# A gated delta rule in front of two expert layers on one Trainium2 core: small transfers on SyncE's queue moved or cut up, unit matrices by memset, more decode buffers, one input placed behind another

## The chip, the cores and the metric

One core of one Trainium2 chip. The metric is the device time of one execution in microseconds (us); the times shown are the median of several runs, and the profile is one execution on its own. Engines: PE is TensorE (PEld its weight loads), DVE VectorE, ACT ScalarE, POOL GpSimd, SP SyncE, which only issues transfers here.

## What is computed

```python
k_n = k / (norm(k) + 1e-6)                       # B=4, H=8, S=768, D=48
for t in range(S):                               # the recurrence, state is [B, H, D, D]
    y[t]  = q[t] @ state
    state = state + beta[t] * outer(k_n[t], v[t] - state @ k_n[t])
x = y as [3072, 384]
p = domain_probs / (domain_probs.sum(-1) + 1e-9)
x = sum over 4 experts e of  p[:, e] * (relu(x @ w1[e]) @ w2[e])       # inner width 1024
out = (sigmoid(x @ w_gate) * (x @ w_val)) @ w_out                      # inner width 1536
```

All inputs and the output are float32.

## The kernel before

**The recurrence in steps.** The sequence is cut into 12 steps of 64 tokens. Inside a step the recurrence is a triangular system, solved with the inverse of a unit triangular matrix per batch and head. Six inversions serve all steps (`INV`): each takes two steps at once, the first two in halves of 32 rows, the other four in full 64. An inversion starts from a unit matrix in `Xpp` (`l_init`, by a transfer from the input `xinit`), reads the triangles from DRAM into `Lpp` (`l_read`), runs pairs of DVE instructions (`itmp`, then `Xpp`; `inv_ops`) and stores its result (`x_out`, tiles `xs` or `xd`). A step's chain (`chain`, `plan_chain`) then reads it into `XT` (`x_in`; `off_in` reads the off-diagonal part into `Ld`), does small products on PE, and leaves its outputs in `YT`. From step 2 on `x_move` carries `YT` into `Y` by eight transfers on SP, two of 144 KB and six of 16 KB, and `x_split` turns `Y` into a rounded part and a rest (`xhi` on ACT, `xlo` on DVE).

**The expert layers.** Tokens go in six batches of two steps (512 columns). A batch passes the four experts ("m1" phases, 8 units of 128 inner columns each) and then the gated layer ("m2", 12 units). Every float32 product is three products of rounded parts. The weights come in tiles of 128x768 on SP (`w_load`, three `raw` buffers), are rounded on ACT and subtracted on DVE into `ws` (`w_split`, four buffers). `finish` multiplies the outputs of an expert with `pe`, the probabilities broadcast to all partitions (`load_p`, two buffers), and adds them in `ACC`, by an accumulating transfer on POOL's queue.

**Decode.** The gated layer's weights arrive as 36 tiles of 64-bit numbers and are turned into float32 once, in the time of the first batch: `dec_load` on SP, `dec_scale` on ACT, `dec_join` on DVE and POOL, `dec_store` on POOL's queue into `w2_d`. `dec_views` picks the buffers: five for the pairs, four (`n % 4`) for the results, all of them parts of tiles that are free at that time (`dec_a`, `dec_b`, `Lpp`, `Xpp`).

**The order.** All instructions are written out in one order by a planner. It counts a time T in planned microseconds that grows by PE's cost of each unit of the expert layers (1.94 for 9 products of 512 columns). Side work has due times on that scale: `plan` puts it into `todo`, decode and inversions go into `back`. `slot` and `fill` emit what is due between units; DVE work only as long as the planned DVE time is at most 2.8 ahead of PE's. Each engine and each queue then runs its own instructions in that order and waits by semaphores. So an instruction on SP that waits holds all transfers behind it, and a queue that waits for nothing runs ahead of PE. `Tile` also lets a transfer wait for the landing of an earlier one whose semaphore it takes over.

Due times around the change: W[1] = 194.6 is when the second batch begins and `g0` for its pair of later steps is W[1] - 116 = 78.6. `plan_norms` loads the keys of steps 4 and 5 from `g0` - 8 on, computes their norms (`norms`) at `g0` + 9 and at once moves them across partitions by four transfers of 4 KB on SP (`norm_move`, tile `nrm_v`). `plan_chain(2, ...)` begins at W[1] - 87 and reads its six inputs 14 before that, after forcing the rest of the second inversion. `x_move(3)` is due at 172.2, `x_split(3)` at 182.6, the read of the third inversion at 168.7. `load_p(n + 2)` follows the last product of phase n.

Of the kernel before, what the change touches and what calls it, by code (L numbers as in the profile page):

```python
# [18 lines left out]
B, H, S, D = 4, 8, 768, 48  # L19
DM = H * D  # L20
# [15 lines left out]
FLIP = 2  # L36
# [4 lines left out]
DEC0, DEC1 = 17.0, 162.0  # L41
# [11 lines left out]
INIT_AT = {}  # L53
_at = 0
for _ng, _n in sorted({inv_cut(r) for r in range(len(INV))}):
    INIT_AT[_ng, _n] = _at
    _at += _n * _n // _ng
# [62 lines left out]
def moe_delta_kernel(  # L120
# [12 lines left out]
    xinit: bass.AP,  # L133
# [112 lines left out]
    def dec_tiles():  # L246
        a = xp.tile([P, KT, 2 * STEP], F32, tag="xhi", name="dec_a").rearrange("p k c -> p (k c)")
        b = xp.tile([P, KT, 2 * STEP], F32, tag="xlo", name="dec_b").rearrange("p k c -> p (k c)")
        w = 2 * DM
        dec_mem.append([a[:, :w], a[:, w:], b[:, :w], Lflat[:, 2 * w : 3 * w], Lflat[:, 3 * w :]])  # L250
        t2 = [b[:, w:], Xflat[:, HC * HC : HC * HC + w]]
        dec_mem.append([t[:, o : o + DM] for o in (0, DM) for t in t2])
        dec_mem.extend([a, b, Lflat[:, 2 * w :]])

    def dec_views(n):
        r, t = dec_mem[0][n % 5], dec_mem[1][n % 4]
        pair = r.bitcast(I32).rearrange("p (a b) -> p a b", b=2)
        return r, pair[:, :, 0], pair[:, :, 1], t
# [226 lines left out]
    def l_init(r):  # L485
        ng, n = inv_cut(r)
        o = INIT_AT[ng, n]
        q[0].dma_start(
            out=x_view(r).rearrange("p j t -> p (j t)"), in_=xinit[:, o : o + n * n // ng]
        )  # L490
# [61 lines left out]
    def x_in(c):  # L552
        r, c2 = INV_OF[c]
        q[2] = nc.sync if c == 2 else q[0]
        xt = XT.rearrange("p h b t -> p (h b) t")
        for i in range(2):
            if INV[r][1]:
                for a in range(2):
                    src = xd_t[r][c2, a, i].rearrange("h b j t -> j (h b) t")
                    put(xt, i * C + a * HC, a * HC, HC, src)  # L560
            else:
                put(xt, i * C, 0, C, xd_t[r][c2, i].rearrange("h b j t -> j (h b) t"))

    def off_in(c):
        r, c2 = INV_OF[c]
        q[2] = nc.sync if c == 2 else q[0]
        if INV[r][1]:
            for bp in range(2):
                src = od_t[r][c2, :, :, bp].rearrange("i h j t -> j (i h) t")
                put(Ld.rearrange("p i h t -> p (i h) t"), bp * C, HC, HC, src)  # L570
# [83 lines left out]
    def x_move(c):  # L654
        dst = Y[c % 2].rearrange("p a f -> p (a f)").rearrange("p (k t) -> p k t", k=KT)
        for o in range(2):
            src = YT[o * C : o * C + D].rearrange("p a i t -> p a (i t)")
            nc.sync.dma_start(out=dst[o * D : (o + 1) * D], in_=src[:, 0:KT])
            for k in range(KT):
                p = 96 + 16 * o  # L660
                nc.sync.dma_start(out=dst[p : p + 16, k], in_=src[16 * k : 16 * k + 16, KT])
# [79 lines left out]
    def plan_norms(c, t):  # L741
        for n in range(2):
            box = []
            plan(t + 9.0 * n, lambda c=c + n, box=box: box.extend(norm_late(c, i) for i in range(2)))
            plan(t + 9.0 * n + 7.0, lambda box=box: [fn() for fn in box])
        plan(t + 17.0, lambda: norms(c, c + 2))

    def norms(c0, c1):
# [17 lines left out]
        if c0:  # L766
            norm_move(c0, c1)
# [172 lines left out]
    inv_done, read_at = [1], {}  # L940
# [29 lines left out]
    def plan_inv(r, tr, t0, t1):  # L970
# [15 lines left out]

        if r == 1:
            read_at[r] = -READ
        else:
            back["inv"].append((tr, "", read, lambda: l_done.issuperset(INV[r][0])))  # L990
# [5 lines left out]
    def plan_chain(c, t, gap):  # L996
# [3 lines left out]
        if c > 1 and c % 2 == 0:  # L1000

            def first():
                while inv_done[0] <= INV_OF[c][0]:
                    back["inv"].pop(0)[2]()
                x_in(c)
                off_in(c)

            plan(t - (14.0 if c == 2 else 13.0), first)
# [5 lines left out]
        if c >= FLIP:  # L1014
            plan(t1 - (2 if c < NC - 1 else 1) * gap + 4.0, lambda: x_move(c))
# [43 lines left out]
    def startup():  # L1059
# [23 lines left out]
        nc.gpsimd.memset(Xflat[:, : HC * HC], 0.0)  # L1083
        nc.gpsimd.memset(Xflat[:, : HC * HC : HC + 1], 1.0)
# [105 lines left out]
        norms(2, 4)  # L1190
        q[1] = None
# [33 lines left out]
    with tc.manual_schedule():  # L1225
# [15 lines left out]
        for k in range(1, NPAIR):  # L1241
# [4 lines left out]
            if k + 1 < NPAIR:  # L1246
                g0 = w - (161.0 if k > 1 else 116.0)
                plan_norms(2 * k + 2, g0 - 8.0)
# [5 lines left out]
            plan_tr(2 * k + 1, w - (TR2 if k > 1 else 12.0), 4.0)  # L1254
# [3 lines left out]
        for what, n, us in EVENTS:  # L1258
            kind, b, e, s0, ns = PHASES[n]
            part = unit_us(kind, ns) / (2 if kind == "m1" else 3)  # L1260
            if what == "b":
# [3 lines left out]
                if us[-1] == (NF1 if kind == "m1" else NF2) - 1 and n + 2 < len(PHASES):  # L1265
                    load_p(n + 2)
# [7 lines left out]
            slot()  # L1274

# [4 lines left out]
def _layouts(q, k, v, beta, moe_domain_probs, moe_w1, moe_w2, moe2_w_gate, moe2_w_val, moe2_w_out):  # L1280
# [43 lines left out]
    init = {}  # L1324
    for ng, n in sorted({inv_cut(r) for r in range(len(INV))}):
        x = np.zeros((ng, P // ng, n // ng, n), f)
        for g in range(ng):
            for j in range(n // ng):
                x[g, :, j, ng * j + g] = 1.0
        init[ng, n] = x.reshape(P, -1)  # L1330
    xinit = np.concatenate(list(init.values()), axis=1)
# [3 lines left out]
        "xinit": xinit,  # L1335
# [20 lines left out]
```

## Time and profile before

| | |
|---|---|
| runs (us) | 1453.33, 1451.38, 1453.0: median 1453.0 |
| profiled execution (us) | 1454.07 |
| its span, first to last instruction (us) | 1452.3 |
| instructions | 25287 |
| busy in the span | PE 1394.3 (96%), PEld 1147.2, DVE 1044.9, ACT 560.8, POOL 241.9 |
| mean granted TensorE clock | 0.974 |
| bytes moved | 246.24 MB, mean 170 GB/s |

The profile's page gives the span, what each engine did in it, and the chain of work that ended last. The trace behind it can be asked for stretches, for one engine's instructions in order of time, and for who ended each wait. A row `X <- Y` in a list of waits says that X stood idle until Y was done; a row of the timeline ends in the idle time before the instruction and its releaser. L148 is a helper through which all DVE instructions go, so DVE is told by tiles. The granted clock is the share of full speed that the chip's throttle gave PE.

### The profile page before, as it was taken

How to read it: one execution, taken by the hardware profiler on the slowest of the kernel's cores; microseconds unless marked ns; L12 is line 12 of the kernel's file. 1: busy time of each engine (PE TensorE's matmuls, PEld its weight loads, DVE VectorE, ACT ScalarE, POOL GpSimd, SP SyncE). 2: the span in 40 equal slices, each digit the busy share in tenths (PEclk: the TensorE clock that was granted, in tenths of full speed). 3: DMA queues.
4: the chain of work that ended last, by engine and by line, in shares of the span. 5: the costliest groups of instructions: out<-in, count | busy, mean ns of one | idle time of the engine just before them, and what ended most of it. 6: DMA issues, size and time to landing. Idle time of an engine off the chain costs nothing.

```text
span 1452.3 us, 25287 instructions
## 1 busy us (share of the span) xinstructions
PE 1394.3 (96%) x9939; PEld 1147.2 (79%) x9939; DVE 1044.9 (72%) x1809; ACT 560.8 (39%) x919; POOL 241.9 (17%) x297
## 2 busy tenths in 40 slices
PE   6879878898999999999999999999999999999998
PEld 5778766787878888878888878888888888888887
DVE  7559887885999677788777788767778755444553
ACT  3335443553332344332344333344433344333343
POOL 2314455660011200001210001210000210000000
PEclk6899998999999999999999999999999999999999
DMA  8876798778446865545775456775434663334331
GB/s 213 236 206 208 218 274 277 233 234 195 155 146 163 212 178 162 161 157 153 196 202 159 138 150 176 189 206 166 127 108 124 155 166 107 131 103 126 99 109 65
DMA packets 115510, 246.24 MB, mean 170 GB/s; under 512 B 38864, under 2 KB 43152, under 8 KB 113216
## 3 DMA queue, kind: packets, MB, share of 16 engines
q1 hardware_dynamic: 94512, 192.24, 43.6%
q0 software_dynamic: 16480, 50.43, 14.7%
q10 hardware_dynamic: 4400, 1.97, 0.6%
q8 instruction: 78, 1.28, 0.4%
q14 instruction: 40, 0.33, 0.1%
HBM read 202.10 MB, written 29.02 MB: 159 GB/s over the span
## 4 chain that ended last, share of the span: by engine, by line
PE 79%; DVE 9%; DMA 7%; issue 2%; ACT 1%; SPq 1%; ACTq 0%; DVEq 0%
PE ph L828 42%; PE acc L865 32%; DVE ws L148 2%; DVE Xpp L148 2%; DVE itmp L148 1%; DMA raw<-in_wp 1%; DMA kn<-in_kt 1%; DMA Y<-YT 1%; PE pu L596 1%; DVE hlo L148 1%; DMA Lpp<-ls 1%; DMA dec_a<-in_wp 1%; PE pk L596 1%; PE pg L373 1%; PE ps L676 1%
## 5 line engine op out<-in xcount | busy, mean ns | idle before, releaser
L828 PE MATMUL ph<-xhi,ws 128*128 128x512 f32 (+1 forms) x2064 | 631.7, 389 | 10.9 <-DVE ws L148 4.9
L865 PE MATMUL acc<-hhi,ws 128*128 128x512 f32 (+1 forms) x1632 | 499.9, 389 | 14.7 <-DVE ctmp L148 6.9
L828 PEld LDWEIGHTS ph<-xhi,ws 128*128 128x128 f32 x2064 | 382.9, 189 | 90.7 <-DVE ws L148 5.8
L828 PE MATMUL ph<-xlo,ws 128*128 128x512 f32 (+1 forms) x1032 | 396.6, 387 | 0.6 <-DVE xlo L148 0.6
L865 PEld LDWEIGHTS acc<-hhi,ws 128*128 128x128 f32 x1632 | 305.1, 190 | 81.1 <-ACT hhi L835 6.1
L148 DVE TENSOR_TENSOR ws<-raw,ws 128x768 fp32r<-128x768 f32 x308 | 302.8, 989 | 47.8 <-ACT ws L229 44.6
L865 PE MATMUL acc<-hlo,ws 128*128 128x512 f32 (+1 forms) x816 | 315.3, 386 | 2.2 <-DVE hlo L148 1.2
L835 ACT ACTIVATE hhi<-ph 128x512 fp32r<-128x512 f32 (+1 forms) x200 | 116.1, 581 | 426.3 <-PE ph L828 421.7
L229 ACT CAST ws<-raw 128x768 fp32r<-128x768 f32 x308 | 252.1, 830 | 62.3 <-DMA raw<-in_wp 51.3
L148 DVE SCALAR_TENSOR_TENSOR hlo<-ph,hhi 128x512 fp32r<-128x512 f32 (+1 forms) x200 | 133.2, 666 | 139.5 <-ACT hhi L835 139.4
L828 PEld LDWEIGHTS ph<-xlo,ws 128*128 128x128 f32 x1032 | 194.9, 189 | 41.4 <-DVE xlo L148 2.5
L865 PEld LDWEIGHTS acc<-hlo,ws 128*128 128x128 f32 x816 | 155.3, 190 | 33.7 <-DVE hlo L148 1.9
L148 DVE TENSOR_TENSOR itmp<-Xpp,Lpp 128x62 f32<-128x62 f32 (+29 forms) x344 | 161.8, 477 | 11.7 <-DMA Lpp<-ls 6.5
L148 DVE TENSOR_TENSOR Xpp<-Xpp,itmp 128x62 f32<-128x62 f32 (+29 forms) x344 | 158.1, 466 | 5.9
L844 ACT CAST hhi<-gv 128x512 fp32r<-128x512 f32 x72 | 44.7, 620 | 164.8 <-DVE gv L148 164.8
L148 DVE TENSOR_TENSOR gv<-ph,sg 128x512 f32<-128x512 f32 x72 | 49.7, 690 | 80.0 <-PE ph L828 76.2
L907 POOL DMA_DIRECT2D ACC<-ctmp x39 | 34.5, 1172 | 366.7 <-DVE ctmp L148 366.6
L148 DVE TENSOR_TENSOR hlo<-gv,hhi 128x512 fp32r<-128x512 f32 x72 | 52.7, 732 | 49.4 <-ACT hhi L844 49.4
L453 POOL DMA_DIRECT2D ld<-LP x12 | 8.1, 678 | 328.0 <-DVE LP L148 232.5
L842 ACT ACTIVATE sg<-ph 128x512 f32<-128x512 f32 x72 | 42.9, 596 | 41.0 <-PE ph L828 40.9
L148 DVE TENSOR_TENSOR ctmp<-acc,pe 128x512 f32<-128x512 f32 (+1 forms) x57 | 35.4, 655 | 10.1 <-PE acc L865 9.3
L581 POOL TENSOR_TENSOR V<-V,nrm_v 128x384 f32<-128x384 f32 x22 | 21.6, 1069 | 42.2 <-DMA V<-in_vt 17.9
(170 smaller groups left out, 927.8 us busy)
## 6 DMA issues: line engine op xcount, KB each, us to landing
raw<-in_wp SPq DMA_DIRECT2D x200, 384.0 KB, 3.3
raw<-w_d SPq DMA_DIRECT2D x108, 384.0 KB, 3.4
ACC<-ctmp POOLq DMA_DIRECT2D x33, 256.0 KB, 5.8
KQ<-in_kg SPq DMA_DIRECT2D x7, 896.0 KB, 7.1
Lpp<-ld POOLq DMA_DIRECT2D x8, 768.0 KB, 14.3
pe<-p_d SPq DMA_DIRECT2D x23, 256.0 KB, 4.7
dec_a<-in_wp SPq DMA_DIRECT2D x15, 384.0 KB, 4.3
Lpp<-in_wp SPq DMA_DIRECT2D x14, 384.0 KB, 6.0
```

The costliest lines, as they stand in the source:

```text
L148: return fn(*args, **kw)
L229: nc.scalar.copy(out=w[:, 0], in_=t)
L373: nc.tensor.matmul(out=pg[i][b * C : (b + 1) * C, j], lhsT=src[b][ROWS[i], 0, h], rhs=src[b][ROWS[i], :, h], start=True, stop=True,)
L581: nc.gpsimd.tensor_tensor(out=V[:, b], in0=V[:, b], in1=nrm_v[:, 2 * c + b].unsqueeze(2).to_broadcast([P, H, D]), op=ALU.mult,)
L596: nc.tensor.matmul(out=ps[r][HALVES[k], h], lhsT=lhsT, rhs=rhs, start=True, stop=True)
L676: nc.tensor.matmul(out=ps[C:112, h], lhsT=KI[0:112, 0, i, h], rhs=rhsA[:, i, h], start=True, stop=True)
L828: nc.tensor.matmul(out=res[q], lhsT=lt, rhs=rt, start=(k == 0 and j == 0), stop=(k == KT - 1 and j == 2))
L835: nc.scalar.activation(out=hh, in_=res[0], func=AF.Relu)
L842: nc.scalar.activation(out=sg, in_=res[0], func=AF.Sigmoid)
L844: nc.scalar.copy(out=hh, in_=gv)
L865: nc.tensor.matmul(out=acc_t[d][:, :w], lhsT=lt, rhs=rt, start=(u == 0 and j == 0), stop=(u == nf - 1 and j == 2),)
L907: nc.gpsimd.dma_start(out=a, in_=t, accum_op=ALU.add)
```

## The change

- `l_init`: the unit matrix of an inversion is written by one memset of zeros and one or two strided memsets of ones on POOL, in place of a transfer; the input `xinit` goes, and with it `INIT_AT`.
- `dec_views`: from tile 8 on the results go round nine buffers, five of them parts of `YQ1`, which step 1 has done with by then.
- `plan_norms`: the first load of keys is due 4 earlier (`g0` - 12), the second stays; `norm_move` leaves `norms` and is due at `g0` + 23 (at the start it follows `norms` as before).
- `plan_chain`, step 2: the second inversion is forced at 30 before the chain in place of 14, and the six inputs (four `XT`, two `Ld`) go on SP one by one, from 23 before the chain on, 2.6 apart.
- `x_move`: four pieces 1.4 apart, the two large transfers first, then the small ones, three and three.
- `plan_inv`: the third inversion's read (`l_init` and `l_read` on POOL's queue) is emitted only once the last piece of `x_move(3)` is emitted and 4 us of PE's planned time have passed.
- `x_split(3)` is due 3 later, 9 in place of 12 before the batch.
- `load_p(n + 1)` follows unit 3 of phase n, for n from 1 on.

```diff
-FLIP = 2
+FLIP, MOVE = 2, 4.0
-DEC0, DEC1 = 17.0, 162.0
+DEC0, DEC1, MORE = 17.0, 162.0, 8
...
+        y = YQ1.rearrange("p a i h t -> p (a i h t)")
+        dec_mem.append([y[:, o : o + DM] for o in range(0, 5 * DM, DM)] + dec_mem[1])
...
-        r, t = dec_mem[0][n % 5], dec_mem[1][n % 4]
+        r, t = dec_mem[0][n % 5], dec_mem[1][n % 4] if n < MORE else dec_mem[5][(n - MORE) % 9]
...
     def l_init(r):
         ng, n = inv_cut(r)
-        o = INIT_AT[ng, n]
-        q[0].dma_start(
-            out=x_view(r).rearrange("p j t -> p (j t)"), in_=xinit[:, o : o + n * n // ng]
-        )
+        w = P // ng
+        nc.gpsimd.memset(Xflat[:, : n * n // ng], 0.0)
+        for g in range(ng):
+            nc.gpsimd.memset(Xflat[g * w : (g + 1) * w, g : n * n // ng : n + ng], 1.0)
...
     def x_move(c):
         dst = Y[c % 2].rearrange("p a f -> p (a f)").rearrange("p (k t) -> p k t", k=KT)
-        for o in range(2):
-            src = YT[o * C : o * C + D].rearrange("p a i t -> p a (i t)")
-            nc.sync.dma_start(out=dst[o * D : (o + 1) * D], in_=src[:, 0:KT])
+        srcs = [YT[o * C : o * C + D].rearrange("p a i t -> p a (i t)") for o in range(2)]
+
+        def most(o):
+            nc.sync.dma_start(out=dst[o * D : (o + 1) * D], in_=srcs[o][:, 0:KT])
+
+        def rest(o):
+            p = 96 + 16 * o
             for k in range(KT):
-                p = 96 + 16 * o
-                nc.sync.dma_start(out=dst[p : p + 16, k], in_=src[16 * k : 16 * k + 16, KT])
+                nc.sync.dma_start(out=dst[p : p + 16, k], in_=srcs[o][16 * k : 16 * k + 16, KT])
+            moved[c] = pe_at[0]
+
+        return [lambda o=o, fn=fn: fn(o) for fn in (most, rest) for o in range(2)]
...
-            plan(t + 9.0 * n, lambda c=c + n, box=box: box.extend(norm_late(c, i) for i in range(2)))
-            plan(t + 9.0 * n + 7.0, lambda box=box: [fn() for fn in box])
-        plan(t + 17.0, lambda: norms(c, c + 2))
+            plan(t + 13.0 * n, lambda c=c + n, box=box: box.extend(norm_late(c, i) for i in range(2)))
+            plan(t + 13.0 * n + 7.0, lambda box=box: [fn() for fn in box])
+        plan(t + 21.0, lambda: norms(c, c + 2))
+        plan(t + 35.0, lambda: norm_move(c, c + 2))
...
-        if c0:
-            norm_move(c0, c1)
...
+        def ready():
+            return l_done.issuperset(INV[r][0]) and (r > 2 or pe_at[0] > moved.get(3, 1e9) + MOVE)
+
-            back["inv"].append((tr, "", read, lambda: l_done.issuperset(INV[r][0])))
+            back["inv"].append((tr, "", read, ready))
...
-                x_in(c)
-                off_in(c)
-
-            plan(t - (14.0 if c == 2 else 13.0), first)
+                if c > 2:
+                    x_in(c)
+
+            def one(n):
+                q[2] = nc.sync
+                put(*(x_parts(c) + off_parts(c))[n])
+
+            plan(t - (30.0 if c == 2 else 13.0), first)
+            for n in range(6 if c == 2 else 0):
+                plan(t - 23.0 + 2.6 * n, lambda n=n: one(n))
...
-            plan(t1 - (2 if c < NC - 1 else 1) * gap + 4.0, lambda: x_move(c))
+            for n, fn in enumerate(x_move(c)):
+                plan(t1 - (2 if c < NC - 1 else 1) * gap + 4.0 + 1.4 * n, fn)
...
-        nc.gpsimd.memset(Xflat[:, : HC * HC], 0.0)
-        nc.gpsimd.memset(Xflat[:, : HC * HC : HC + 1], 1.0)
+        l_init(0)
...
+        norm_move(2, 4)
...
-                plan_norms(2 * k + 2, g0 - 8.0)
+                plan_norms(2 * k + 2, g0 - 12.0)
...
-            plan_tr(2 * k + 1, w - (TR2 if k > 1 else 12.0), 4.0)
+            plan_tr(2 * k + 1, w - (TR2 if k > 1 else 9.0), 4.0)
...
-                if us[-1] == (NF1 if kind == "m1" else NF2) - 1 and n + 2 < len(PHASES):
-                    load_p(n + 2)
...
+            if us[0] == 3 and 0 < n < len(PHASES) - 1:
+                load_p(n + 1)
```

`x_parts` and `off_parts` are the new lists from which `x_in` and `off_in` issue, with the same sources and targets as before.

## Rows read from the trace of the kernel before

**Rows 1.** Stretches: width; busy PE, PEld, DVE, ACT, POOL; granted clock; DMA share, GB/s.

```profile
207.00:219.00 12.00, 7.61 (x25) 5.84 (x26) 11.90 (x16) 3.94 (x7) 11.16 (x11) 0.86 0.97 240
239.00:253.00 14.00, 9.81 (x26) 6.55 (x25) 10.70 (x16) 5.69 (x11) 6.74 (x8) 0.63 0.56 195
275.00:284.00 9.00, 5.81 (x47) 4.69 (x43) 5.75 (x7) 6.66 (x13) 8.55 (x12) 0.81 0.89 295
341.00:352.00 11.00, 6.39 (x19) 4.76 (x18) 4.94 (x9) 4.08 (x6) 0.00 (x0) 0.69 0.95 216
100.00:350.00 250.00, 224.27 (x1759) 183.67 (x1758) 193.18 (x325) 117.61 (x212) 121.76 (x137) 0.95 0.77 233
350.00:475.00 125.00, 124.14 (x648) 100.85 (x648) 118.64 (x212) 43.93 (x69) 11.74 (x16) 1.00 0.54 155
525.00:1450.00 925.00, 922.52 (x5804) 757.46 (x5802) 634.33 (x1000) 346.75 (x537) 71.26 (x92) 1.00 0.51 146
```

**Rows 2.** PE in order of time: start, us, instruction, [idle before it, releaser].

```profile
78.28 0.45 PE L596 MATMUL pk<-rhsA,KS 48*64 48x48 f32 x2 [4.64 <-DVE rhsB L148]
...
213.73 0.70 PE L865 MATMUL acc<-hhi,ws 128*128 128x512 f32 x2 [4.19 <-DVE ctmp L148]
...
242.09 1.19 PE L865 MATMUL acc<-hhi,ws 128*128 128x512 f32 x2 [2.31 <-DVE ws L148]
...
278.90 0.91 PE L828 MATMUL ph<-xhi,ws 128*128 128x512 f32 x2 [3.19 <-DVE ws L148]
...
346.16 1.22 PE L828 MATMUL ph<-xhi,ws 128*128 128x512 f32 x2 [4.61 <-ACT sg L842]
```

**Rows 3.** PE's waits from 100 to 350: total us, times, longest.

```profile
PE acc L865 <- DVE ws L148: 5.9, 4, 2.3
PE ph L828 <- DVE ws L148: 4.9, 2, 3.2
```

**Rows 4.** The chain that ended last, in order of time: start, us, what.

```profile
66.31 8.89 DMA Lpp<-ls
...
188.31 12.51 DMA kn<-in_kt
...
206.98 3.44 DMA dec_a<-in_wp
...
235.48 4.75 DMA w_d<-dec_b
...
269.59 6.48 DMA w_d<-Xpp
...
328.56 15.99 DMA Y<-YT
```

**Rows 5.** Waits of SP's queue (143:150, 195:205) and of ACT (whole span).

```profile
SPq L806 <- DVE itmp L148: 5.9, 1, 5.9
...
SPq L774 <- DVE norm_tmp L148: 8.0, 1, 8.0
...
ACT xhi L669 <- DMA Y<-YT: 11.2, 1, 11.2
...
ACT dec_b L268 <- DMA w_d<-dec_b: 2.7, 1, 2.7
```

**Rows 6.** Transfers issued: tiles, queue, count, KB each, median us to landing.

```profile
Xpp<-in_xinit SPq DMA_DIRECT2D x1, 512.0 KB, 7.2
```

**Rows 7.** Groups of POOL's instructions: count, busy us, mean ns, idle before.

```profile
L1083 POOL MEMSET Xpp<- 128x1024 f32 x1 | 1.0, 951 | 0.3 <-POOLq L1343 0.3
```

**Rows 8.** POOL in order of time, from 318 to 330.

```profile
323.64 0.56 POOL L488 DMA_DIRECT2D Xpp<-in_xinit  x1 [3.14 <-DMA w_d<-Xpp]
```

**Rows 9.** DVE in order of time, from 214 to 217.

```profile
215.55 2.65 DVE L148 TENSOR_TENSOR ws<-raw,ws 128x768 fp32r<-128x768 f32 x1
```

**Rows 10.** POOL in order of time, from 214 to 219.

```profile
215.73 3.15 POOL L581 TENSOR_TENSOR V<-V,nrm_v 128x384 f32<-128x384 f32 x2
```

**Rows 11.** Instructions that write or read `itmp`, by stretch: DVE busy (count), clock, DMA.

```profile
350.00:362.00 12.00, 5.74 (x18) 0.96 0.49 150
```

More of the change, by code (lines that the diff above doesn't have):

```diff
@@ L50, in inv_cut @@
     return ((2 if small else 4) // len(steps), HC if small else C)
[L53 to L57, printed above, removed]
 INV_OF = {c: (r, steps.index(c)) for r, (steps, _) in enumerate(INV) for c in steps}
@@ L132, in moe_delta_kernel @@
     mask: bass.AP,
-    xinit: bass.AP,
     out: bass.AP,
@@ L550, in put, with x_parts @@
         q[2].dma_start(out=t[p0 : p0 + n, :, c0 : c0 + n], in_=src)
-    def x_in(c):
+    def x_parts(c):
         r, c2 = INV_OF[c]
-        q[2] = nc.sync if c == 2 else q[0]
         xt = XT.rearrange("p h b t -> p (h b) t")
+        parts = []
         for i in range(2):
@@ L559, in x_in, with off_parts @@
                     src = xd_t[r][c2, a, i].rearrange("h b j t -> j (h b) t")
-                    put(xt, i * C + a * HC, a * HC, HC, src)
+                    parts.append((xt, i * C + a * HC, a * HC, HC, src))
             else:
-                put(xt, i * C, 0, C, xd_t[r][c2, i].rearrange("h b j t -> j (h b) t"))
-    def off_in(c):
+                parts.append((xt, i * C, 0, C, xd_t[r][c2, i].rearrange("h b j t -> j (h b) t")))
+        return parts
+    def off_parts(c):
         r, c2 = INV_OF[c]
-        q[2] = nc.sync if c == 2 else q[0]
+        parts = []
         if INV[r][1]:
@@ L569, in off_in, with x_in @@
                 src = od_t[r][c2, :, :, bp].rearrange("i h j t -> j (i h) t")
-                put(Ld.rearrange("p i h t -> p (i h) t"), bp * C, HC, HC, src)
+                parts.append((Ld.rearrange("p i h t -> p (i h) t"), bp * C, HC, HC, src))
+        return parts
+    def x_in(c):
+        q[2] = q[0]
+        for part in x_parts(c):
+            put(*part)
+    def off_in(c):
+        q[2] = q[0]
+        for part in off_parts(c):
+            put(*part)
     def scale_v(c):
@@ L939, in moe_delta_kernel @@
     back = {"dec": [], "inv": []}
-    inv_done, read_at = [1], {}
+    inv_done, read_at, moved = [1], {}, {}
     turn_ = [""]
@@ L1323, in _layouts @@
     mask = np.tile(np.triu(np.ones((C, C), f), 1), (2, 1))
[L1324 to L1331, printed above, removed]
     return {
@@ L1334, in _layouts @@
         "wp2": np.ascontiguousarray(wp2).view(np.int64), "ident": ident, "mask": mask,
-        "xinit": xinit,
     }
```

## The prediction

> **What bounds the kernel now.** The page shows TensorE (PE) as the engine that is never long idle, so I read PE by stretches. From 525 to 1450 it is busy for 922.52 of 925.00 us at a granted clock of 1.00: nothing can be won there. From 100 to 350 it is busy for 224.27 of 250.00 us at 0.95, that is 25.7 us idle and about 12.5 us (0.05 of 250) lost to the lower of its two clock levels, 1.2 instead of 2.4 GHz: some 38 us that an edit could win there at most [rows 1]. Half clock follows each idle stretch, so I price a stall as idle time plus (1 - granted) x width: 207:219 costs 4.39 + 1.68 = 6.1 us, 239:253 4.19 + 5.18 = 9.4, 275:284 3.19 + 1.71 = 4.9, 341:352 4.61 + 3.41 = 8.0 [rows 1]. PE's own instructions in order of time name the releaser of each: VectorE (DVE) or ScalarE (ACT), never PE [rows 2]; the list of its waits there sums the smaller ones [rows 3]. The chain of waits leads one step further back, to transfers [rows 4], and the waits of SyncE's queue (SP) and of ACT tell why those were late [rows 5].
>
> **The change, part by part.**
>
> *Unit matrices by memset.* For the second inverse SP issued 512 KB of `xinit`, 7.2 us to landing [rows 6], just ahead of `Lpp<-ls`, which took 8.89 us from 66.31, to 75.20 [rows 4]. Without it `Lpp<-ls` takes its place: 7.2 us from some 65.7 is 72.9, about 2.3 us earlier. DVE waits for this landing and PE then 4.64 us for DVE's `rhsB` [rows 2]. I take 2.3 us and a little of the half clock behind it: **3.0**; bounds 0 (the weight tile behind it may come no sooner) and 4.6. The memsets: 951 ns for 1024 columns [rows 7], so about 1.0 us for the small form and 1.9 for the large, on POOL, behind the same stores for which the transfer waited; before the third inverse POOL was idle for 3.14 us [rows 8]. Cover: the read of the triangle, far longer, goes beside or behind it. What it could cost is DVE's time: while POOL ran its product `V<-V,nrm_v`, one `ws` subtraction took 2.65 us [rows 9, 10]: that much per memset at the very worst, within PE's reserve there; I take 0. The Trainium skill, "SBUF — State Buffer", section "Who interferes with whom", says that a VectorE instruction with two SBUF inputs contends with a GpSimd instruction that reads SBUF and not with one that only writes it: by that rule the memsets, which only write, cost DVE 0, by the row up to 2.65 us each; no row of before has a memset beside such work.
>
> *`load_p` at the fourth unit of a phase.* Each of the 25 loads of `pe` stays; its place moves. It waited on SP for DVE to finish with the buffer, 5.9 us before 149.06 [rows 5] and much the same a phase later, with weight loads queued behind. PE's four waits for `ws` in `acc` products make 5.9 us, 2.3 of them in 239:253, so 3.6 for the three others [rows 3]. The new place comes after the phase's last products: the wait goes, the 256 KB stay. **1.5**; bounds 0 and 3.6.
>
> *`norms` and `norm_move` apart, norm loads 13 apart.* Per pair of steps four tiny transfers waited on SP for DVE's norms, 8.0 us before 204.21 [rows 5]. Behind them stood a decode load and a weight load; the chain runs `kn<-in_kt` 12.51, norms, these four, `dec_a<-in_wp` 3.44, ACT, DVE, and ends in the 4.19 us at 213.73 [rows 2, 4]. Moved 14 planned us later, they find the norms done. The earlier norm load no longer finds its buffer taken. The last three pairs lie where PE has no idle time: 0. I take **6.0** of the 6.1 us of 207:219; bounds 2 and 7.8 (of the 4.9 us that `ph` products waited for `ws`, 1.7 lie just ahead, at 207 [rows 3]).
>
> *Step 2's input in six pieces, earlier.* Six transfers leave the crowd at 209 to 217 on SP and go between weight loads from 84.6 planned us on. Added wait: the first needs the second inverse stored; weight loads queue behind it, and PE behind these. Its forced end moves from 93.6 to 77.6 planned us, against a planned 78.0, so it pulls in two or three small DVE steps. Bounds: 1 us of gain (six issues out of the crowd) and 6 of loss (what the norms' wait costs at the same place); taken 0, since both the store and its readers move forward.
>
> *Five more decode buffers.* Tile n waits on ACT until tile n - 4 is stored; weight casts stand behind it. Chain: `w_d<-dec_b` 4.75 us from 235.48, then ACT, DVE, PE at 242.09; `w_d<-Xpp` 6.48 us from 269.59, then PE at 278.90 [rows 2, 4]. With nine buffers the store has five tiles more. But the weight tiles behind land only a little before, so the next wait is a load. Of 9.4 + 4.9 us I take 6 + 4 = **10**; bounds 2.7 (what ACT itself waited for the first store [rows 5]) and 14.3.
>
> *Step 3: `x_move` in pieces, split 3 planned us later, third inverse's input behind it, no 1 MB `xinit`.* The last `Y<-YT` took 15.99 us from 328.56 [rows 4]; ACT stood 11.2 us before the cast [rows 5], and PE waited 4.61 us [rows 2]. Beside it POOL's queue held 1 MB of `xinit`, 1.5 MB of `Lpp<-ld` and 0.5 MB of `YQ<-pd` (sizes by the tiles' shapes). One of these 3 MB goes, the split comes one gate unit and a down product of PE's work later (by the planner's costs 5.8 us), and pieces let weight loads between. **7.5** of 8.0; bounds 2 and 8. That wait of ACT's is the only one of its kind in the span: in the later batches x has reserve, which the pieces shorten by some 3 us: 0.
>
> *Price of that delay.* The third inverse's read is due at 168.7 before and at some 181 now (last piece of x at 176.4, and 4): 12 planned us later. Its steps' first 12 us held 5.74 us of DVE work [rows 11], while DVE is busy for 118.64 of 125.00 us from 350 to 475: 6.4 us spare [rows 1]. It just fits, ahead of step 4's chain. I take **-2.0**; bounds 0 and -8.
>
> Not touched: the start up to 60, and a stall near 146 behind DVE's own decode and inverse work.
>
> Sum: 3.0 + 1.5 + 6.0 + 10.0 + 7.5 - 2.0 = 26. Stalls stand in a row, and a PE that no longer waits reaches the next one earlier, so I keep 22. The profiled execution took 1454.07 us (span 1452.3 and 1.8 around it), 1.07 over the median of 1453.0: 1432 on its scale, **1431** as a median. A measurement of this kernel can tell 0.2%, 2.9 us, from no change.
>
> **Rivals.**
>
> *The third inverse's input does not go behind x.* The new condition orders the program, but POOL waits for nothing of PE's there: its read went out from 323.64 on, as soon as the last store had landed [rows 8]. With memset, `Lpp<-ld` would start at some 326, amid the pieces of x, and only the missing 1 MB helps. For it: those issue times. Against: the later split gives 5.8 us of reserve. Part of the last term falls, 7.5 to 2: 1431 + 5.5 = 1436.5. The Trainium skill, "DMA: Bandwidth & Descriptors", section "Queues, rings and completion order", has each DMA engine take turns between queues packet by packet, so place in one queue gives no precedence over another; the trace agrees, as `Y<-YT` stayed slow while POOL's transfers ran.
>
> *Bytes, not order, are late.* From 207 to 219 the DMA engines are busy at 0.97 [rows 1]; then unblocking SP only lengthens landings. Norm term 6 to 2, decode term 10 to 3 (its lower bound): 1431 + 11 = 1442. Against: 0.56 in 239:253 [rows 1].
>
> *Slower: DVE becomes the bound behind 350.* If the 6.4 us of spare are gone because decode, pressed into fewer us, also ends late, the lag of the third inverse shows at each place where PE waits for a stage's last products: three phase ends to 475 and step 4's chain. Four times 6.4 us and a clock drop of 1.7 is 32; 1431 - 2 (the term already in) + 32 = 1461. It decides from a lag of about 3.9 us per place on, where four such losses eat 22. For: 118.64 of 125.00 us. Against: PE is busy for 124.14 of the same 125.00 [rows 1], so such ends cost next to nothing now, and the planner holds DVE's work to 2.8 us ahead of PE.
>
> *No change*: what is won before 350 is lost again there, 1453.
>
> **Numbers.** Forecast 0.53 (alone 1424 to 1438), input not behind x 0.20, bytes 0.15, slower 0.05, no change 0.04, still better (every bound at its good end, some 1420) 0.03. Faster 0.91, same 0.04, slower 0.05. The range 1421 to 1445 holds the forecast and two rivals with their bounds and leaves out the last three and a little more.
>
> **What would show it.** Right: no wait of `nrm_v` on SP over 1 us before 210; no ACT wait for `w_d` after 200; 207:219, 239:253 and 275:284 without their stalls; no ACT wait over 2 us for `Y<-YT`; `Lpp<-ls` about 2 us sooner; 350 to 475 at a PE load as now. Wrong: new PE waits for DVE's `ctmp` or `ACC` behind 350, waits for weight tiles in place of the removed ones, or SP held by `XT<-xs`.

## The result, and the profile after

The changed kernel takes 1440.05 us (median of 4 runs, 1437.62 to 1443.21), the kernel before 1453.16 in the same lot: ratio 0.991, 95% interval 0.9884 to 0.9936. Run again later it gave 1441.08 (6 runs; ratio 0.9921, 0.9898 to 0.9944). All ten together have a median of 1441.1, and that is what the experiments are held against; 61 runs of the kernel before, over all lots, have one of 1453.8. So the change is worth 12.7 us, 0.9%. Forecast were 22. Single runs of one kernel lie up to some 8 us from its median (before: 1447.33 to 1461.61), so differences are given with twice their standard error, from the means.

The profiled execution took 1437.62 us (span 1435.6). Its stretches, with the columns of [rows 1]; the first four are those of [rows 1] where a stall was, shifted by what PE is ahead:

```profile
199.00:211.00 12.00, 7.80 (x28) 6.00 (x27) 11.86 (x17) 4.65 (x8) 10.91 (x12) 0.86 0.89 210
229.00:243.00 14.00, 9.22 (x27) 6.43 (x26) 11.73 (x16) 5.24 (x11) 8.72 (x9) 0.76 0.62 221
264.00:273.00 9.00, 8.23 (x94) 6.67 (x93) 7.84 (x12) 7.51 (x14) 7.55 (x10) 1.00 1.02 346
330.00:341.00 11.00, 11.00 (x49) 8.89 (x49) 6.44 (x8) 5.01 (x8) 0.00 (x0) 1.00 0.88 256
100.00:350.00 250.00, 232.48 (x1743) 189.48 (x1743) 203.45 (x338) 122.77 (x218) 125.64 (x139) 0.97 0.79 238
350.00:475.00 125.00, 123.46 (x645) 99.76 (x644) 120.91 (x216) 40.00 (x62) 15.92 (x20) 1.00 0.50 146
480.00:530.00 50.00, 49.52 (x596) 40.27 (x597) 35.49 (x62) 22.20 (x35) 9.15 (x13) 1.00 0.83 191
```

Priced as the prediction did (idle plus clock): 199:211 still costs 4.20 + 1.68 = 5.9 us, where 6.1 stood before; 229:243 costs 4.78 + 3.36 = 8.1, where 9.4 stood; 264:273 costs 0.8 and not 4.9; 330:341 nothing and not 8.0. **Two of the four stalls are gone, the two ahead of them are nearly untouched.** PE in order of time, as in [rows 2]:

```profile
205.22 1.19 PE L878 MATMUL acc<-hhi,ws 128*128 128x512 f32 x2 [4.20 <-DVE ctmp L142]
...
232.56 0.70 PE L878 MATMUL acc<-hhi,ws 128*128 128x512 f32 x2 [1.80 <-DVE ws L142]
...
237.27 0.79 PE L878 MATMUL acc<-hlo,ws 128*128 128x512 f32 x1 [2.86 <-DVE hlo L142]
...
267.04 0.74 PE L841 MATMUL ph<-xhi,ws 128*128 128x512 f32 x2 [0.77 <-DVE ws L142]
```

The wait for `ctmp` at 205.22 has the very length of that at 213.73 in [rows 2]. DVE in order of time tells why it is late:

```profile
189.19 0.68 DVE L142 SCALAR_TENSOR_TENSOR hlo<-ph,hhi 128x512 fp32r<-128x512 f32 x1
192.90 1.10 DVE L142 TENSOR_REDUCE w_all<-kn 128x8 f32<-128x384 f32 x2 [3.02 <-ACT kn L748]
...
197.68 0.95 DVE L142 TENSOR_TENSOR ws<-raw,ws 128x768 fp32r<-128x768 f32 x1
...
201.16 1.22 DVE L142 TENSOR_TENSOR LP<-LP,w_all 128x1024 f32<-128x1024 f32 x1
202.29 1.58 DVE L142 TENSOR_TENSOR ws<-raw,ws 128x768 fp32r<-128x768 f32 x1
...
204.40 1.87 DVE L142 TENSOR_TENSOR ctmp<-acc,pe 128x512 f32<-128x512 f32 x3
```

DVE stands 3.02 us for ACT's square of `kn`, and from 192.90 on it has no gap over 0.3 us until `ctmp` is done: norms, decode, `LP` scaling and weight tiles follow one another. The kernel before did the same, 8.6 us later, and PE came 8.5 us later there:

```profile
201.47 1.07 DVE L148 TENSOR_REDUCE w_all<-kn 128x8 f32<-128x384 f32 x2 [1.86 <-ACT kn L734]
```

ACT waits for the transfer (its waits from 100 to 350 in the changed kernel):

```profile
ACT kn L748 <- DMA kn<-in_kt: 3.4, 1, 3.4
```

And SP's queue has a new wait (from 143 to 235):

```profile
SPq L546 <- DMA xs<-Xpp: 6.9, 1, 6.9
```

SP no longer waits for the norms (8.0 us in [rows 5]), nor for DVE ahead of `pe` near 146. But it stands 6.9 us, from 184.8 to 191.7, for the store of the second inverse, the wait that step 2's earlier pieces add; weight loads stand behind it. The transfers issued from 178 to 184 are slow too (tiles, queue, count, KB each, median us to landing):

```profile
LP<-raw_d SPq DMA_DIRECT2D x1, 1024.0 KB, 11.6
...
kn<-in_kt SPq DMA_DIRECT2D x2, 192.0 KB, 12.9
```

Stretches by the DMA engines' share (the column before the last; the view's count can exceed 1) show that they are full there, and were not before 170:

```profile
120.00:170.00 50.00, 46.97 (x265) 41.05 (x264) 46.35 (x87) 24.26 (x44) 26.55 (x29) 0.97 0.68 221
170.00:180.00 10.00, 10.00 (x46) 8.29 (x45) 9.93 (x21) 6.55 (x12) 4.95 (x7) 1.00 1.07 270
180.00:190.00 10.00, 8.68 (x39) 6.87 (x38) 9.63 (x17) 3.05 (x5) 7.63 (x8) 1.00 1.02 305
190.00:200.00 10.00, 9.82 (x44) 7.82 (x43) 6.46 (x18) 6.16 (x13) 3.55 (x4) 1.00 1.07 367
...
220.00:230.00 10.00, 10.00 (x104) 8.16 (x103) 6.61 (x13) 4.82 (x9) 5.85 (x7) 1.00 1.00 374
```

So two explanations stood against each other for what stayed: **ORDER** (SP held for `xs`, the loads behind it late) and **BYTES** (full DMA engines: what is unblocked lands late all the same).

### The profile page after: what moved, and what is told of

Read it like the earlier page. It is cut to its first block, busy times and chain, and to the rows that moved or that the text cites. A ratio compares the mean times of both kernels' runs of the same rounds, so it can differ in the third digit from the quotient of the medians.

```text
span 1435.6 us, 25281 instructions
## 1 busy us (share of the span) xinstructions
PE 1389.4 (97%) x9939; PEld 1143.0 (80%) x9939; DVE 1047.7 (73%) x1809; ACT 560.6 (39%) x919; POOL 254.2 (18%) x307
## 4 chain that ended last, share of the span: by engine, by line
PE 78%; DVE 12%; DMA 5%; issue 3%; ACT 1%; POOL 0%; ACTq 0%; DVEq 0%; SPq 0%
PE ph L841 41%; PE acc L878 32%; DVE ws L142 2%; DVE Xpp L142 2%; DVE itmp L142 2%; DVE hlo L142 1%; DMA dec_a<-in_wp 1%; PE pu L604 1%; PE ps L690 1%; PE pg L369 1%; PE yt L646 1%; PE pk L604 1%; DMA Lpp<-in_wp 1%; PE yt L647 1%; DMA raw<-in_wp 1%
```

## Experiments

Every kernel is the changed one with the edit shown; each was timed beside the kernel before. Not all lots ran on the same chip. The kernel before has means of 1453.0 to 1454.6 us in them, and the differences given leave that in.

### Two large loads moved out of the full stretch (e1_lp_early)

```
-  plan(t, lambda: nc.sync.dma_start(out=LP[c % 2], ...))
+  plan(t - (35.0 if c == 4 else 56.0), lambda: nc.sync.dma_start(out=LP[c % 2], ...))
```

> Two 1 MB loads of LP (steps 4 and 5) are issued 35 and 56 planned us earlier, at some 135 to 150 us, where the DMA engines are busy at 0.5 to 0.65, and not at 179 and 218, where they are busy at 1.0. Nothing else moves, SP still waits for the store of the second inverse (xs) before the first piece of step 2's input. Theory BYTES (between 170 and 235 the DMA engines are full, so whatever is unblocked lands late): the norm loads kn land by 190 and not at 192.9, the stall of PE for ctmp at 201 falls from 4.2 us to 2 or less, the two stalls at 231 and 234 (1.8 and 2.9) together to 3 or less; total 3 to 6 us below the changed kernel's 1440, that is 1434 to 1437. Theory ORDER (SP held 7 us by the wait for xs is what kept the stall): the stall at 201 stays at 3.5 us or more, total 1439 to 1441.

Measured: 1435.67 us (6 runs; ratio 0.9881, 0.9856 to 0.9906), 4.4 ± 2.7 below the changed kernel. A wait of 1.2 us is all that is left of the stall (PE's waits from 198 to 225):

```profile
PE acc L878 <- ACT YQ L264: 1.2, 1, 1.2
```

The list puts the wait down to ACT, but DVE's first `ctmp` ends within 0.04 us of ACT's `YQ`: DVE is as late, and from 187 on it has no gap over 0.3 us ahead of `ctmp`. The two loads, now issued at 138.0 and 143.1, took 5.5 and 6.8 us to land in place of 11.6 and 6.7, and from 190 to 200 the share is 0.93 and not 1.07. SP still waits for `xs`, as it did, so ORDER did not hold the stall up. One number of BYTES failed: `kn` landed at 191.7 and 192.8, not by 190. How far the start has come is told here by ACT's ninth weight cast: 102.4 in this execution, 97.9 in the changed kernel's profile, 102.1 in its second one (below). Against that second profile, whose start is alike, `kn` landed some 3 us sooner, and DVE no longer stood for it. The two stalls at 231 and 234 became one of 3.2 us.

### Step 2's input back in its old place (e2_pieces_back)

```
-  plan(t - (30.0 if c == 2 else 13.0), first)
-  for n in range(6 if c == 2 else 0):
-      plan(t - 23.0 + 2.6 * n, lambda n=n: one(n))
+  plan(t - (14.0 if c == 2 else 13.0), first)    # first() issues all six
```

> Step 2's input goes back to its old place (six transfers in a row, 14 planned us ahead of its chain), the rest of the change stays. Theory ORDER: SP no longer stands from 184.7 to 191.7, the weight loads behind go out about 7 us sooner, the stall at 201 falls from 4.2 us to 1.5 or less; total 1434 to 1437. Theory BYTES: the loads go out sooner and land no sooner than about 2 us before, the stall stays between 3 and 5 us; total 1438 to 1442. The prediction's term for this part is 0, with bounds of 1 us of gain and 6 of loss for the pieces.

Measured: 1439.95 us (6 runs, 1433.44 to 1444.11; 0.9902, 0.9874 to 0.9929), 2.1 ± 3.7 below: nothing that can be told from none. The stall near 201 is still there:

```profile
PE acc L878 <- DVE ctmp L142: 3.2, 1, 3.2
```

With no wait for `xs` on SP, 3.2 us of the stall stay; the changed kernel's two profiles have 4.2 and 2.9. ORDER falls as its main cause.

### Four decode buffers again (e3_four_buffers)

```
-DEC0, DEC1, MORE = 17.0, 162.0, 8
+DEC0, DEC1, MORE = 17.0, 162.0, 1000000
```

> The decoded tiles have four buffers again, not nine, the rest of the change stays. The prediction's term: 10 us lost, 1450. Theory BYTES (the tiles that come with nine buffers find their loads late): 2 to 4 us lost, 1442 to 1444, the waits of ACT for w_d are back at 220 to 275.

Measured: 1447.24 us (12 runs; 0.9957, 0.9939 to 0.9975), 5.9 ± 1.9 above the changed kernel. The loss lies behind 260, in these waits of PE from 260 to 340, which in the changed kernel are 2.5 us in all:

```profile
PE ph L841 <- DVE ws L142: 4.4, 2, 2.6
PE ph L841 <- ACT sg L855: 2.2, 2, 1.6
```

In 222:260 this kernel loses 4.1 us of idle time and 3.4 of clock, the changed one 5.3 and 3.4, in its second profile 4.6 and 1.5. The buffers do their work at the third stall and behind it, not at the second.

### The norms as before (e4_norms_back)

```
-  plan(t + 13.0 * n + ...)          # load, then 7.0 later the squares
-  plan(t + 21.0, lambda: norms(c, c + 2))
-  plan(t + 35.0, lambda: norm_move(c, c + 2))
+  plan(t + 9.0 * n + ...)
+  plan(t + 17.0, lambda: (norms(c, c + 2), norm_move(c, c + 2)))
...
-  plan_norms(2 * k + 2, g0 - 12.0)
+  plan_norms(2 * k + 2, g0 - 8.0)
```

> norms and norm_move are together again and the norm loads of a pair 9 planned us apart, as before; the rest of the change stays. The prediction's term: 6 us lost, 1446. Theory BYTES: 1 to 3 us lost, 1441 to 1443, and the stall for ctmp near 201 stays within 1.5 us of 4.2. SP waits again about 8 us for DVE's norms ahead of the four nrm_v transfers.

Measured: 1437.5 us (6 runs; 0.9894, 0.9873 to 0.9915), 3.2 ± 1.6 **below** the changed kernel. Both theories had expected a loss. The stall is no longer than in the changed kernel:

```profile
PE acc L877 <- DVE ctmp L142: 2.5, 1, 2.5
```

But SP's wait for the norms is back at 2.7 us only, not at the expected 8 (and `kn`'s loads wait 3.6 us for their buffer again). The last experiment below, which undoes this part among others, has it back in full, and a stall of 3.5 us, within the 2.3 to 4.2 of the kernels that leave the `LP` loads in place (SP's waits from 165 to 215 there):

```profile
SPq L786 <- DVE norm_tmp L142: 8.4, 1, 8.4
```

So SP's wait for the norms was not what held PE. Why the whole is 3 us faster is not settled; between 480 and 530 this profile loses nothing, where the changed kernel's two lose 0.5 and 1.6.

### The changed kernel again (after_again)

> The changed kernel itself once more, for its spread and a second profile. The kernels with one part undone reached their ninth weight cast 0.1 to 2.3 us ahead of the profile of before, the changed kernel's own profile 5.1 us ahead, though its start-up is theirs. Theory START (the start varies by some us from execution to execution): median 1438 to 1441, this profile's ninth cast lies 0 to 3 us ahead of before, and the stall for ctmp near 201 is smaller than 4.2 us by about as much as the start is later, since the loads behind it land by their own count. Rival: the 5.1 us are the memset's and come again within 0.5 us.

Measured: 1441.08 us (1439.77 to 1444.17). The ninth cast came at 102.1, 0.9 us ahead of the profile of before; the stall near 201 is 2.9 us. So the start does vary by 4 us from one execution to the next, and of these two the later one meets the shorter stall. DVE's wait for `kn` makes that difference: 3.0 us in the first profile, 1.6 in the second. In all but one of the ten profiles that leave the `LP` loads in place, the stall is that wait (1.0 to 3.0 us) plus 1.2 to 1.8 us; in e6_loadp_back DVE stands 4.4 us for decode besides, and the stall is 4.2. The 5.1 us by which the first profile was ahead at 103 are not the memset's alone.

### Step 3's x and the third inverse as before (e5_third_back)

```
-  for n, fn in enumerate(x_move(c)):
-      plan(t1 - (2 if c < NC - 1 else 1) * gap + 4.0 + 1.4 * n, fn)
+  plan(t1 - (2 if c < NC - 1 else 1) * gap + 4.0, lambda: [fn() for fn in x_move(c)])
...
-  return l_done.issuperset(INV[r][0]) and (r > 2 or pe_at[0] > moved.get(3, 1e9) + MOVE)
+  return l_done.issuperset(INV[r][0])
...
-  plan_tr(2 * k + 1, w - (TR2 if k > 1 else 9.0), 4.0)
+  plan_tr(2 * k + 1, w - (TR2 if k > 1 else 12.0), 4.0)
```

> Step 3's split 3 planned us sooner again, its x moved in one go, the third inverse's input without its condition; the unit matrix is still a memset. The prediction's terms: 7.5 lost and 2 won back, 1445.5, and the stall of 4.6 us near 335 is back with its half clock. Rival (the 1 MB that no longer moves beside Y<-YT is what cleared the place): stall of 2 us or less there, total 1440 to 1442. The wait of ACT for Y<-YT tells them apart: over 8 us by the first, under 4 by the second.

Measured: 1435.66 us (6 runs; 0.9884, 0.9861 to 0.9907), 5.0 ± 1.8 **below** the changed kernel. The stall at step 3's x does not come back; ACT's wait for it is 4.0 us, where 11.2 stood in [rows 5]:

```profile
ACT xhi L683 <- DMA Y<-YT: 4.0, 1, 4.0
```

The rest of the change clears the place without this part, and what it takes away there is the 1 MB of the unit matrix. (One thing stays of the part: the two large transfers of x go ahead of the six small ones. What that does by itself was not tried.) POOL in order of time shows the rest; first the changed kernel, then this one:

```profile
313.06 1.81 POOL L484 MEMSET Xpp<- 128x2048 f32 x1 [3.49 <-DMA w_d<-Xpp]
314.93 0.36 POOL L486 MEMSET Xpp<- 64x32 f32 x2
315.43 1.05 POOL L493 DMA_DIRECT2D Lpp<-ld  x2
...
471.95 2.25 POOL L543 DMA_DIRECT2D xd<-Xpp  x2 [17.54 <-DVE Xpp L142]
481.85 1.65 POOL L546 DMA_DIRECT2D XT<-xd  x2 [7.65 <-issue]
483.49 1.83 POOL L484 MEMSET Xpp<- 128x2048 f32 x1
```

```profile
314.76 1.07 POOL L493 DMA_DIRECT2D Lpp<-ld  x2 [0.17 <-issue]
...
463.05 2.25 POOL L543 DMA_DIRECT2D xd<-Xpp  x2 [10.93 <-issue]
...
474.10 1.68 POOL L546 DMA_DIRECT2D XT<-xd  x2 [7.13 <-issue]
```

The third inverse's input starts at 315.43 with the condition and at 314.76 without: the condition does not put it behind x, whose last pieces SP issues from 317.38 to 321.13. It puts only DVE's share later in program order, and the inverse is stored at 471.95 and not at 463.05 (466.06 with the condition alone taken out, below). `XT<-xd` for step 4 then lands at 490.0 (second profile: 492.1) and not at 479.1, just where PE wants it. In the changed kernel's first profile PE waits 0.5 us there, in its second 1.6:

```profile
492.19 1.02 PE L604 MATMUL pu<-R,XT 64*64 64x48 f32 x55 [1.59 <-DMA XT<-xd]
```

That is not all of the 5.0 us; where the rest was is not shown.

### The load of `pe` back behind a phase's last unit (e6_loadp_back)

```
+  if us[-1] == (NF1 if kind == "m1" else NF2) - 1 and n + 2 < len(PHASES):
+      load_p(n + 2)
...
-  if us[0] == 3 and 0 < n < len(PHASES) - 1:
-      load_p(n + 1)
```

> The load of pe goes back behind a phase's last unit, the rest of the change stays. The prediction's term: 1.5 us lost (bounds 0 to 3.6), 1442.5 against the changed kernel's 1441 (10 runs of two lots). SP waits again 4 us or more for DVE ahead of pe near 145 and 168, and the waits of PE for ws in acc products around 156 to 190 grow by 1 us or more together. Rival (weight tiles have reserve over that wait): within 1 us of 1441, waits for ws as they are, 1.3 to 2.3 us.

Measured: 1443.91 us (11 runs; 0.9937, 0.9916 to 0.9958), 4.3 ± 2.4 above by the means and 2.8 by the medians. SP waits 5.9 and 5.7 us ahead of `pe` again, and PE, from 150 to 210, 4.8 us in `acc` products for `ws` (1.3 in the changed kernel's second profile):

```profile
PE acc L878 <- DVE ws L142: 4.8, 3, 1.8
```

### The unit matrices from memory again (e7_xinit_back)

```
-  nc.gpsimd.memset(Xflat[:, : n * n // ng], 0.0)
-  for g in range(ng): nc.gpsimd.memset(Xflat[g * w : (g + 1) * w, g : n * n // ng : n + ng], 1.0)
+  q[0].dma_start(out=x_view(r)..., in_=xinit[:, o : o + n * n // ng])
```

> The unit matrices of the second and later inverses come from memory again (512 KB and 1 MB), all else as in the changed kernel. The prediction's term: 3 us lost for the second inverse, and part of the 7.5 at the third if the 1 MB beside x matters: 1443 to 1446. Theory START (the gain seen at 60 to 100 us is mostly the start's own spread): 1440 to 1442, with Lpp<-ls landing within 2 us of where the changed kernel's later starts have it, and the place near 340 still without a stall over 1 us.

Measured: 1445.36 us (9 runs; 0.9942, 0.9922 to 0.9962), 4.4 ± 1.5 above. No stall of PE near 340: moving x later clears that place without the memset too. The loss has no one place. At step 4's input the 1 MB for the fourth inverse now goes out amid `XT<-xd`, but PE's wait for that is what the changed kernel's second profile has too (PE's waits from 475 to 530):

```profile
PE pu L610 <- DMA XT<-xd: 1.7, 1, 1.7
PE acc L884 <- DVE hlo L148: 1.4, 1, 1.4
```

Against that second profile PE is idle 1.7 us longer from 222 to 260, 1.1 from 100 to 195, 1.0 from 480 to 530 and 0.8 from 325 to 365.

### Loads for the norms earlier as well (e8_lp_kn_early)

To the first experiment's edit:

```
+  early = 11.0 if c == 4 else 0.0
-  plan(t + 13.0 * n, ...)                      # load
-  plan(t + 13.0 * n + 7.0, ...)                # squares
+  plan(t - early + 13.0 * n, ...)
+  plan(t + 13.0 * n + 7.0 - early * (1 - n), ...)
```

> e1_lp_early and, besides, the two loads of step 4's and step 5's keys for the norms 11 planned us sooner; the squares of step 5 stay where they are. Theory BYTES (DVE stands for kn, which lands late behind a full DMA, and is then late for ctmp): kn lands before ACT asks for it, DVE no longer idles 3 us ahead of the norms, no stall over 1 us between 185 and 215; total 1432 to 1436, at or below e1_lp_early's 1435.7. Rival (DVE is full there by its own work): a stall for DVE of 1.5 us or more stays near 205, total as e1_lp_early, 1435 to 1437.

Measured: **1434.52 us** (6 runs, 1432.40 to 1435.74; 0.9873, 0.985 to 0.9896), 6.6 ± 1.6 below the changed kernel, the fastest version of this study. `kn` lands at 176.2 and 178.1, and DVE no longer stands for it. The list shows no wait for `ctmp` near 205 (PE's waits from 185 to 260):

```profile
PE acc L879 <- DVE hlo L142: 3.2, 1, 3.2
PE acc L879 <- ACT YQ L264: 1.3, 1, 1.3
```

Against the first experiment it wins 1.1 us of median, within the spread. A wait of 1.3 us stays, over the 1 us that BYTES allowed. It is put down to ACT's decode, which ends at 206.87; but DVE's first `ctmp`, for which PE also waits, ends at 206.86, and DVE has no gap over 0.3 us ahead of it. So what is left is DVE's own work as much: the rival had the cause, if not its 1.5 us. Of the 6.6 us, 0.5 to 1.6 lie from 480 to 530, where this profile loses nothing, though the edit moves nothing there.

### The condition alone taken out (e9_ready_back)

```
-  ... and (r > 2 or pe_at[0] > moved.get(3, 1e9) + MOVE)
```

> Only the new condition on the third inverse's input is taken out; x of step 3 still moves in pieces and its split stays 3 planned us later. Theory LATE END (the input starts on POOL's queue at the same time with and without the condition, 314 to 316 us; what the condition delays is DVE's share, so that the third inverse is stored at 472 and not at 463, and XT<-xd for step 4 lands at 490 to 492, where PE wants it): xd<-Xpp is issued at 462 to 466, no wait of PE for XT<-xd, no loss between 480 and 530, total 1435 to 1438. Rival (it is the pieces or the later split that cost what e5_third_back won): 1440 to 1442, xd<-Xpp at 470 or later.

Measured: 1439.45 us (4 runs; 0.9898, 0.9879 to 0.9917), 1.5 ± 1.6 below. The profile does what LATE END said: the third inverse is stored at 466.06, and from 480 to 530 PE waits for nothing. The time hardly does: 1.5 us and not 3 to 6 (2.7 if each kernel is held against the kernel before of its own lot). The rest of what the experiment that undid the whole part won is then with the pieces or the later split, or chance; that is not settled.

### Both gains together (e10_lp_kn_third)

The edits of e8_lp_kn_early and e5_third_back in one kernel.

> e8_lp_kn_early (1434.5) with e5_third_back's undoing of the third inverse's part as well (which alone took the changed kernel from 1441 to 1435.7). If LATE END and BYTES are separate losses, both gains add up but for what e8's profile did not lose at 480 to 530: 1430 to 1433. If they are one loss shown in two places: 1434 to 1436.

Measured: 1434.94 us (4 runs, 1431.8 to 1435.92; 0.9864, 0.9844 to 0.9884). The gains do not add up. The two losses are not separate ones, or not both there in one execution. And the stall for `ctmp` is there again, though `kn` had landed by 175.7 and DVE has no gap over 0.3 us from 187 to 205 (PE's waits from 185 to 260):

```profile
PE acc L879 <- DVE ctmp L142: 2.2, 1, 2.2
```

This start was some 3 us ahead of the two before it (ninth cast at 99.7, e1_lp_early 102.4, e8_lp_kn_early 103.1). So with `kn` in time DVE's own work is what PE meets here, and a PE that comes sooner waits longer for it.

### Three parts alone (e11_three_parts)

Norms, step 2's input and step 3's part are undone together (the edits above); memset, `load_p` and nine buffers stay.

> Only three parts of the change are kept: unit matrices by memset, the load of pe at the fourth unit, nine decode buffers. Norms, step 2's input and step 3's x with the third inverse are as before. If the parts' own undoings add up (1437.5, 1439.95 and 1435.7 against 1441: 3.5, 1 and 5.4 won), 1431; if the same few us were counted more than once (a PE that comes sooner waits longer at the next place), 1434 to 1437. By the prediction's terms, which give those parts 6.0, 0 and 7.5 - 2.0 of gain, 1441 + 11.5 = 1452.5, and the stall of 4.6 us at step 3's x is back. No stall of PE over 1 us near 335 to 350 and none from 480 to 530 if the memset alone clears the one and the earlier end of the third inverse the other.

Measured: 1437.12 us (6 runs; 0.9885, 0.9861 to 0.9909), 3.5 ± 1.9 below the changed kernel. **Three of the six parts give all of the gain and some us more.** The gains of single undoings do not add up to 1431 here either. Its stretches 330:341 and 480:530 show no stall at either place, the one with the memset alone, the other with the earlier end:

```profile
330.00:341.00 11.00, 11.00 (x50) 9.11 (x49) 9.66 (x23) 4.73 (x8) 0.00 (x0) 1.00 0.73 175
480.00:530.00 50.00, 50.00 (x620) 40.83 (x619) 35.46 (x64) 21.55 (x35) 5.33 (x8) 1.00 0.70 186
```

## Why the prediction was right and where it was wrong

It had the direction, and 1440.05 lies in its range; 22 us were forecast, some 13 came. That the range reaches that far is due to the rival "bytes, not order" (1442), not to the forecast's own terms. By its steps:

*Unit matrices by memset, 3.0.* Right in its mechanism: `Lpp<-ls` landed at 70.8 and 69.6, not at 75.2 [rows 4]. Undone it costs 4.4 ± 1.5 us, but that brings back 1 MB for each later inverse too, the fourth's at step 4's input, which the prediction did not name; how much is won at 66 itself the spread of the start hides. The memsets cost DVE nothing, as taken (below).

*`load_p`, 1.5.* Under-sized: 2.8 to 4.3, still about its upper bound of 3.6.

*`norms` and `norm_move` apart, 6.0.* **This step failed.** "Moved 14 planned us later, they find the norms done" came true, SP no longer waits. The chain was read wrongly one step back. Behind its 12.51 us of `kn<-in_kt` [rows 4] DVE had no gap from 201.47 on until `ctmp` in the kernel before: the decode load behind the four small transfers held ACT there (3.5 us), not DVE. In the changed kernel `kn` lands 8.5 us sooner and PE is 8.5 us ahead, so the stall has its old length. It has two parts: DVE's wait for `kn` (1.0 to 3.0 us) and DVE's own work behind that. The three kernels that move 2 MB out of the full stretch are rid of the first and keep 1.2, 1.3 and 2.2 us. That these are DVE's own work is read from its timeline; no experiment took work off it. So at most some 3 of the 6.0 us hung on a transfer at all, and none showed: undoing this part is 3.2 ± 1.6 us faster.

*Step 2's input, 0.* The wait on SP came, 6.9 us, but the 6 us of loss that the bound had set for PE did not: undoing the part wins 2.1 ± 3.7 us, so 0 stands.

*Five decode buffers, 10.* Right in mechanism, over-sized: 5.9 ± 1.9. The 4 at 275:284 came (4.9 to 0.8 there). The 6 of 239:253 did not: 9.4 became 8.1, and in the second profile all of 222:260 still loses 6.1. "The next wait is a load" was written and then not priced.

*Step 3's part, 7.5, and the price of its delay, -2.0.* The 8.0 us of 341:352 did go, so the sum was met; but they go with the memset and the old due times (e5_third_back) as well as with the move and the transfer of the unit matrix (e7_xinit_back), and one price was taken for both together. The first rival was right about the mechanism (the input does not go behind x) and wrong about its price. The delay's price, -2, was right as a number within its bounds and wrong as a place: 350 to 475 is within 0.7 us as busy as before, and what loss there is to see, 0.5 and 1.6 us, is where step 4 loads its input at 490. Undone as a whole the part is 5.0 ± 1.8 us faster; most of that has no place in the profiles.

*The rival "bytes, not order"* (norms 2, buffers 3; 1442) came nearest in time. It was put down for the share of 0.56 in 239:253 [rows 1]. But the decode loads that DVE waits for at the second stall were issued ahead of it, from 220 to 230, at a share of 1.00; that this is why the second stall stays is argued, not shown. Not all of the rival held: the buffers gave 6 and not 3. The slower rival, DVE as the bound behind 350, did not come: PE is busy for 123.46 of 125.00 us there, DVE for 120.91.

*The haircut* from 26 to 22 ("stalls stand in a row") was the right thought and too small: two of the terms, 6.0 and 7.5 - 2.0, are better left out altogether. The six parts undone one at a time sum to some 4 us, and the change is worth 12.7: the parts share stalls, and no single undoing prices one.

Of the signs named in advance these came: no `nrm_v` wait on SP, no wait of ACT of over 0.3 us for `w_d`, none for `Y<-YT`, `Lpp<-ls` sooner by over 4 us, 350 to 475 nearly unchanged, 275:284 without its stall. These did not: 207:219 and 239:253 keep theirs, and SP is held by `XT<-xs`, one of the signs of a failure.

## What to carry to other kernels

A wait that a queue shows is worth its length only if the transfers behind it land sooner without it, and if the engine that needs them then has time: look for the last gap of that engine ahead of the stall, for what ended it, and count the engine's own work from there on. Look at the DMA engines' share not at the stall but over the stretch in which the late transfer was issued; where it is near 1, moving bytes to a stretch that still had room (0.63 from 130 to 150 here) helped where moving issues did not. When two edits clear the same stall, give its price once. A condition in program order delays only engines that read that order in step; a queue that runs ahead starts when its own waits end, so check the start time there before counting on the delay.

## What the hardware showed that was not expected

A share near 1 does not tell how long a transfer takes to land: the same 1 MB `LP` load took 11.6 us from 179 on in the changed kernel (share 1.02 from 180 to 190) and 6.8 us from 143 on in the first experiment, with the DMA engines as full:

```profile
140.00:150.00 10.00, 7.53 (x49) 6.51 (x48) 9.93 (x21) 3.84 (x8) 7.51 (x9) 1.00 0.99 379
```

And "full" is not a rate: at a share of 1.0 or more the changed kernel moved between 270 and 374 GB/s in stretches of 10 us. Why the one load was faster is not shown.

A memset on POOL cost DVE nothing here. DVE's instructions beside the memset that runs from 313.06 to 314.87:

```profile
314.01 0.69 DVE L142 TENSOR_TENSOR hlo<-gv,hhi 128x512 fp32r<-128x512 f32 x1 [0.69 <-ACT hhi L857]
314.75 0.96 DVE L142 TENSOR_TENSOR xlo<-Y,xhi 128x768 fp32r<-128x768 f32 x1
```

They take what they take alone (0.69 us for the first form at 310.33 too, with no memset beside it). So does a `ws` subtraction wholly beside the second inverse's memset: 0.95 us at 55.97. The `ws` subtraction that DVE started at 207.05, of the form that takes 0.95 at 197.68, took 2.65 us beside POOL's product, which reads two operands, as in [rows 9]:

```profile
207.05 2.65 DVE L142 TENSOR_TENSOR ws<-raw,ws 128x768 fp32r<-128x768 f32 x1
```

The Trainium skill, "SBUF — State Buffer", section "Who interferes with whom", has it so: a VectorE instruction with two SBUF inputs contends with a GpSimd instruction that reads SBUF and not with one that only writes it. The trace agrees on both (2.65 us beside the product, 0.69 and 0.95 beside the memsets).

Two executions of the same kernel can show the start at different clocks and yet reach the same place. The stretch 0:60 of the changed kernel's first and second profile:

```profile
0.00:60.00 60.00, 41.01 (x688) 35.18 (x689) 44.53 (x168) 20.53 (x47) 14.46 (x24) 0.73 0.87 234
```

```profile
0.00:60.00 60.00, 44.43 (x634) 38.15 (x638) 44.72 (x168) 19.99 (x45) 14.46 (x24) 0.99 0.87 231
```

At a granted clock of 0.99 the first weight cast came 0.5 us later (50.7 against 50.2) than at 0.73: in these two PE's clock did not bound the start. The DMA engines have the same share of 0.87 in both.
